# Sparse attention and two MLPs on one core: k and q split once per pair of heads and placed by DMA, x scaled by turned row sums, an order made with slack

## The chip, the cores and the metric

The kernel runs on one core of one Trainium2 chip. The core has TensorE (PE, with its weight loads PEld), VectorE (DVE), ScalarE (ACT), GpSimd (POOL) and SyncE (SP), which issues every DMA here. The metric is the device time of one execution in microseconds; lower is better. Before the change it is 1143.46 us, the median of three runs (1141.05 to 1149.29).

## The reference, cut to what matters

All is in float32, for 4 batches of 8 heads, 576 tokens and head width 64. The result of the attention, 2304 tokens by 512, goes through two MLPs of inner width 2048.

```python
scores = (1.0 / np.sqrt(64)) * np.matmul(q, k.transpose(0, 1, 3, 2))
thresh = np.max(scores, axis=-1, keepdims=True) - tau
scores = np.where(scores >= thresh, scores, -1000000000.0)
attn = np.exp(scores - np.max(scores, axis=-1, keepdims=True))
attn = attn / (np.sum(attn, axis=-1, keepdims=True) + 1e-09)
x = np.matmul(attn, v)                     # then heads side by side: 2304 x 512
h = x @ moe_w_in                           # 512 -> 2048
x = np.where(h > 0.0, h, np.exp(np.minimum(h, 0.0)) - 1.0) @ moe_w_out
h = x @ moe2_w_in
out = np.maximum(0.01 * h, h) @ moe2_w_out
```

## The kernel before, in words

**Exact products from two halves.** TensorE multiplies float32 slowly (two records for each matmul in the trace) and fp32r, a shortened float32, fast. So most operands are split into a high half, which is the value as fp32r, and a low half, the value less its high half. A weight, an activation or an attention weight is then multiplied in two or three fast matmuls. The first heads are not split: up to head `P32` = 9 (not included) the product with v, and up to head `Q32` = 8 the product of q and k, are done in plain float32 (`pv32`, `qk32`).

**Units.** The 32 heads go in 16 pairs. A pair has 9 units of 128 rows of queries: A0 to A3 of its first head, M with the last 64 rows of both heads, and B2, B3, B0, B1 of its second. A unit makes its scores in PSUM tile `s` (in the first 41 units, every other one in `y`), in two halves of 288 keys (L462 in float32, L469 split). VectorE scales them, copies them to `ss` and finds the row's extreme (L477), `thr` is made by VectorE (L482) or POOL (L480), ScalarE masks (L486) and takes the exponential with its row sum `su` (L489, then a read of the sum), VectorE takes the reciprocal (L491), and ScalarE (L306) or POOL (L304) multiplies the whole 128x576 tile `e` by it. TensorE turns `e` in four pieces (L501) and a rest of 64 keys, shared by two units (L516). The turned weights are copied (L568, L569) or split (L546, L549, L553, L556) into `wh`, `wl` and `lt`. When a window of 256 or 320 queries of a head is complete, `pv32` (L587) or `pv` (L606) multiplies with v: nine matmuls for a window, since v's halves lie side by side and give two results in the two halves of PSUM tile `v`.

**After pv.** One half of `v` is copied to `tm`, the other to `x`, each by ScalarE or VectorE, and POOL adds `tm` to `x` (L614, shown under its helper's line L300).

**The halves of k and q.** From head 8 on, `head` loads k and q twice, into both halves of the 128 partitions (L408). POOL makes the high half of k (`k1`, L304) and the low half (`k2`, L300), the high half of q and, in partitions 64 to 127, the low half (L304, L300), for each head anew.

**The first MLP beside the attention.** Six blocks of 256 tokens go through half of the first MLP (8 of 16 slices of the inner width) while the attention of later batches runs (`block` with `reg=True`: L647 makes h, L657 to L674 the activation and its split, L688 y). A block needs x of all heads of its batches (`xready`). The sixteen weight tiles for it are split into halves by POOL, ScalarE and VectorE in the same stretch (L257 to L286). After about 476 us only the MLPs are left, mostly with 512 tokens in a matmul.

**What sets the order.** `Order` is a list scheduler in the program: each operation has a due time (`vt`, in units of `TU`, with offsets in `ST0` and `ST1`), one or more engines that may do it with a cost for each, and the operations and buffers that it waits for. It plays these out once, and what comes out is the fixed order of each engine's queue. On the chip each queue runs in that order: an instruction that waits holds up all that stand behind it on its engine, and SP's queue of DMAs likewise.

## Time and profile before

| | |
|---|---|
| median of three runs | 1143.46 us |
| the profiled execution: its time, its span | 1140.95 us, 1139.2 us |
| PE, PEld busy | 1112.0 us, 940.5 us |
| DVE, ACT, POOL busy | 721.1 us, 665.1 us, 375.9 us |
| granted TensorE clock, mean over the span | 0.993 |
| chain that ended last, shares of the span | PE 76%, ACT 11%, DVE 9%, issue 2%, POOL 1% |
| DMA | 71.52 MB, mean 63 GB/s |

How to read it: busy is the time in which an engine has at least one record open. TensorE's records overlap, since the next matmul starts long before the last record ends, so PE shows 98% although it does not start a matmul as often as it could. What TensorE really loses is seen from the starts of the matmuls: the time from one start to the next, against the shortest time that the same matmul needs when nothing holds it up. The other engines' records do not overlap. The span falls into three stretches: float32 attention alone (to about 124 us), attention with the first MLP beside it (to about 476 us), and the MLPs alone.

### The profile page before, as it was taken

What the parts mean: (1) busy time and instruction counts of PE and PEld (TensorE: products, weight loads), DVE (VectorE), ACT (ScalarE), POOL (GpSimd) and SP (SyncE); (2) the same over time, 40 slices, a digit from 0 to 9 for tenths busy, and PEclk for the clock granted to TensorE, in tenths of its full rate; (3) what the DMA queues carried; (4) which work ended last, traced back from release to release, by engine and by line L of the source; (5) the groups of instructions that cost most, each with busy time, mean ns of one, the idle gap of its engine ahead of it and who ended that gap; (6) DMA issues with size and microseconds to landing.
All of it is one profiled execution on the core that took longest, in us unless ns stands there. A gap on an engine that the chain in (4) does not pass through costs nothing.

```text
span 1139.2 us, 17486 instructions
## 1 busy us (share of the span) xinstructions
PE 1112.0 (98%) x6312; PEld 940.5 (83%) x6312; DVE 721.1 (63%) x1633; ACT 665.1 (58%) x1391; POOL 375.9 (33%) x485
## 2 busy tenths in 40 slices
PE   8999999999999999999999999999999999999998
PEld 4555588999989998889888888988888888888898
DVE  5878788888888887678888643886332322322332
ACT  5888899999999999556545332554322222322222
POOL 3546788889779877101001010010000000000000
PEclk8999999999999999999999999999999999999999
DMA  6333122212122211234434200331010010010010
GB/s 166 108 108 107 37 62 62 84 48 80 52 63 69 81 50 29 75 127 135 161 116 125 93 10 28 93 112 56 1 38 1 1 37 1 1 37 1 1 38 20
DMA packets 37366, 71.52 MB, mean 63 GB/s; under 512 B 9760, under 2 KB 17312, under 8 KB 37280
## 3 DMA queue, kind: packets, MB, share of 16 engines
q1 hardware_dynamic: 37280, 70.40, 20.3%
q8 instruction: 50, 0.82, 0.3%
q14 instruction: 36, 0.29, 0.1%
HBM read 60.95 MB, written 9.44 MB: 62 GB/s over the span
## 4 chain that ended last, share of the span: by engine, by line
PE 76%; ACT 11%; DVE 9%; issue 2%; POOL 1%; POOLq 0%; DVEq 0%; ACTq 0%
PE y L688 31%; PE h L647 16%; PE hb L647 14%; PE v L587 4%; ACT e L489 3%; PE t L501 3%; ACT ss L486 3%; DVE ss L477 2%; PE s L469 2%; ACT wh L546 2%; PE v L606 2%; PE s L462 1%; PE y L462 1%; DVE wl L549 1%; DVE g L659 1%
## 5 line engine op out<-in xcount | busy, mean ns | idle before, releaser
L688 PE MATMUL y<-gh,woh 128*128 128x512 f32 (+1 forms) x736 | 256.8, 349 | 1.6 <-ACT ys L568 1.6
L688 PE MATMUL y<-gl,woh 128*128 128x512 f32 (+1 forms) x736 | 252.3, 343 | 0.0
L688 PE MATMUL y<-gh,wol 128*128 128x512 f32 (+1 forms) x736 | 252.1, 343 | 0.0
L647 PE MATMUL h<-xh,wih 128*128 128x256 f32 (+1 forms) x464 | 157.1, 338 | 3.9 <-DVE g L665 3.6
L688 PEld LDWEIGHTS y<-gh,woh 128*128 128x128 f32 x736 | 139.4, 189 | 18.6 <-ACT ys L568 2.2
L647 PE MATMUL h<-xl,wih 128*128 128x256 f32 (+1 forms) x464 | 153.2, 330 | 0.0
L647 PE MATMUL h<-xh,wil 128*128 128x256 f32 (+1 forms) x464 | 153.1, 330 | 0.0
L688 PEld LDWEIGHTS y<-gl,woh 128*128 128x128 f32 x736 | 139.3, 189 | 16.2
L688 PEld LDWEIGHTS y<-gh,wol 128*128 128x128 f32 x736 | 139.0, 189 | 16.2
L672 ACT CAST gh<-g 128x512 fp32r<-128x512 f32 (+1 forms) x184 | 97.1, 528 | 86.2 <-DVE g L670 46.9
L300 POOL TENSOR_TENSOR xl<-x,xh 128x256 fp32r<-128x256 f32 (+1 forms) x30 | 24.2, 820 | 342.4 <-ACT xh L625 342.4
L299 DVE TENSOR_TENSOR gl<-g,gh 128x512 fp32r<-128x512 f32 (+1 forms) x132 | 85.3, 647 | 54.8 <-ACT gh L672 53.5
L486 ACT ACTIVATE ss<-ss,thr 128x576 f32<-128x576 f32 x144 | 111.5, 775 | 5.8 <-DVE thr L482 3.7
L489 ACT ACTIVATE e<-ss,taun 128x577 f32<-128x577 f32 x144 | 112.0, 778 | 1.5
L477 DVE TENSOR_SCALAR_CACHE_REDUCE ss<-s,scl 128x576 f32<-128x576 f32 x124 | 100.8, 813 | 9.8 <-PE s L462 5.2
L647 PEld LDWEIGHTS h<-xh,wih 128*128 128x128 f32 x464 | 88.1, 190 | 14.4 <-DVE g L665 3.7
L647 PE MATMUL hb<-xl,wih 128*128 128x512 f32 (+1 forms) x272 | 99.1, 364 | 0.0
L647 PE MATMUL hb<-xh,wih 128*128 128x512 f32 (+1 forms) x272 | 99.0, 364 | 0.0
L647 PE MATMUL hb<-xh,wil 128*128 128x512 f32 (+1 forms) x272 | 99.0, 364 | 0.0
L469 PE MATMUL s<-k,qt 128*128 128x288 f32 x472 | 86.6, 306 | 8.4 <-DVE ss L477 8.1
L647 PEld LDWEIGHTS h<-xh,wil 128*128 128x128 f32 x464 | 87.8, 189 | 8.2
L647 PEld LDWEIGHTS h<-xl,wih 128*128 128x128 f32 x464 | 87.7, 189 | 8.1
(538 smaller groups left out, 2124.8 us busy)
## 6 DMA issues: line engine op xcount, KB each, us to landing
wraw<-in_w1i_dram SPq DMA_DIRECT2D x16, 512.0 KB, 4.2
wraw<-in_w1o_dram SPq DMA_DIRECT2D x16, 512.0 KB, 3.5
wraw<-in_w2i_dram SPq DMA_DIRECT2D x16, 512.0 KB, 3.5
wraw<-in_w2o_dram SPq DMA_DIRECT2D x16, 512.0 KB, 3.5
kraw<-in_kT_dram SPq DMA_DIRECT2D x48, 160.0 KB, 2.9
qraw<-in_qT_dram SPq DMA_DIRECT2D x48, 144.0 KB, 2.8
ys<-yp_dram SPq DMA_DIRECT2D x4, 1024.0 KB, 5.5
out_dram<-x SPq DMA_DIRECT2D x16, 256.0 KB, 2.1
```

What stands on the lines that cost most here:

```text
L299: return pick(who, D=(dve(n), lambda: nc.vector.tensor_tensor(**args()), PORT), P=(pool_tt(n), lambda: nc.gpsimd.tensor_tensor(**args())))
L300: P=(pool_tt(n), lambda: nc.gpsimd.tensor_tensor(**args())))
L462: nc.tensor.matmul(s()[n * w:n * w + w, j, 0:HALF], q()[0:64, c:c + w], k()[0:64, k0 + j * HALF:k0 + (j + 1) * HALF], start=True, stop=True)
L469: nc.tensor.matmul(s()[:, j, 0:HALF], q()[:, c:c + 128], kk()[:, k0 + j * HALF:k0 + (j + 1) * HALF], start=(n == 0 and m == 0), stop=(n == ...
L477: o = op((DVE, dve(S) + 60, lambda: nc.vector.tensor_scalar(out=ssr().rearrange("p (j c) -> p j c", j=2), in0=s()[:, :, 0:HALF], scalar1=s ...
L486: o = op((ACT, act(S) + 95, lambda: nc.scalar.activation(out=ssr(), in_=ssr(), func=AF.Prelu, bias=thr(), scale=-1.0, alpha=STEEP)), [ot], ...
L489: o = op((ACT, act(S) + 190, lambda: nc.scalar.activation(out=er(S + 1), in_=ssr(S + 1), func=AF.Exp, bias=taun, accum_out=su())), [o], [s ...
L501: nc.tensor.transpose(t4()[:, c, :], er()[:, c1 + c * 128:c1 + (c + 1) * 128], ident)
L587: nc.tensor.matmul(ps()[0:64, 0:nw], lhs, rhs, start=(c == 0), stop=(c == 4))
L647: nc.tensor.matmul(hp(), w_()[:, cs], x_()[:, 0:tb], start=(k == 0 and z == 0), stop=(k == KC - 1 and z == 2))
L672: o1 = op((ACT, act(tb), lambda: nc.scalar.copy(out=gh()[:, cs], in_=g()[:, cs])), [o], [g, gh], vt)
L688: nc.tensor.matmul(ysl(yg, m), w_()[:, cs], g_()[:, 0:tb], start=(first and z == 0 and share == 0), stop=(last and z == 2 and end))
```

## The change

- `Q32` goes from 8 to 4: heads 4 to 7 also get split k and q.
- k and q of a pair of heads are loaded together into 128 partitions (`kq_pair`), split once by POOL, the low half in place, and twelve DMAs from SBUF to SBUF place the halves where the matmuls want them.
- `e` is no longer multiplied by the reciprocal of its row sum. The sums of a pair's nine units are collected in one tile `su`; TensorE turns it to 9x128, VectorE takes the reciprocal, one DMA stores it in DRAM, three DMAs read it back spread over 64 partitions each, and one 128x576 multiplication by VectorE or POOL scales the pair's part of `x`.
- After `pv`, one half of PSUM tile `v` is copied to `x`, and VectorE adds the other half from PSUM. `tm` is gone.
- In the scheduler an operation of TensorE counts as ready 49.7 ns later, those of the other three engines cost 30 ns more, and latencies count 1.31 times. All due times have other values.

```diff
-P32, Q32 = 9, 8
+P32, Q32 = 9, 4
...
-KN = dict(warm=3, TU=2691.9, hlead=0.875114, hleadb=3.14713, wv0=3.2304, wv1=2.45697, yoff=28639.7, coff=-5493.3,
+KN = dict(margin=49.6784, pad=30.0, late=1.30757, plead=2.02161, warm=3, TU=2594.9, hlead=-1.09928,
+          hleadb=1.51858, wv0=3.7208, wv1=4.27865, yoff=32778.1, coff=-7939.5, NS=41, vlate=-5075.7,
...
-                t = max((d.done + hop(d.eng, e) for d in o.deps), default=0.0)
+                t = max((d.done + hop(d.eng, e) for d in o.deps), default=0.0) + (KN["margin"] if e == PE else 0.0)
...
+            if e in (ACT, DVE, POOL):
+                cost += KN["pad"]
...
+    def kq_pair(p, vt):
+        kr, qr, kh, qh = kraw_r.new(), qraw_r.new(), kh_r.new(), qh_r.new()
+        vt -= KN["plead"] * TU
+        parts = []
+        for r, h, src, n in ((kr, kh, kT, SL), (qr, qh, qT, S)):
+            ld = op((SP, 600, lambda r=r, src=src: nc.sync.dma_start(
+                out=r(), in_=src[2 * p:2 * p + 2].rearrange("g d s -> (g d) s"))), [], [r], vt - 3000, lat=3500)
+            oh = op(hi_of("P", n, h, r), [ld], [r, h], vt)
+            ol = op(tt("P", n, lambda r=r, h=h: dict(
+                out=r().bitcast(F32R), in0=r(), in1=h().bitcast(F32), op=ALU.subtract)), [oh], [r, h], vt)
+            parts.append((oh, ol))
+        (okh, okl), (oqh, oql) = parts
+        for j in range(2):
+            k1, k2, q = k1_r.new(), k2_r.new(), qt_r[j].new()
...
+            for dst, at, cs, src, raw, o in (
+                    (k1, 0, slice(0, SL), kh, 0, okh), (k1, 64, slice(0, SL), kh, 0, okh),
+                    (k2, 0, slice(0, SL), kr, 1, okl), (k2, 64, slice(0, SL), kr, 1, okl),
+                    (q, 0, qs, qh, 0, oqh), (q, 64, qs, qr, 1, oql)):
+                deps.append(op((SP, 600, lambda dst=dst, at=at, cs=cs, src=src, raw=raw, mine=mine: nc.sync.dma_start(
+                    out=dst()[at:at + 64, cs].bitcast(F32), in_=src()[mine] if raw else src()[mine].bitcast(F32))),
+                    [o], [src, dst], vt + 1500 + 5 * TU * j, lat=3000))
...
-        o = op((DVE, 75, lambda: nc.vector.reciprocal(out=rs(), in_=su())), [o], [su, rs], vt + so["rec"])
-        o = op(hi_of("PA", S, er, er, rs), [o], [e, rs], vt + so["norm"])
...
+    def row_sums(p, vt):
+        (su, done), rb, rt, ps = sums.pop(p), rb_r.new(), rt_r.new(), v_ps.new()
+        o = op((PE, 107, lambda: nc.tensor.transpose(ps()[0:NU, 0:128], su(), ident)), done, [su, ps], vt)
+        o = op((DVE, dve(128), lambda: nc.vector.reciprocal(out=rt(), in_=ps()[0:NU, 0:128])), [o], [ps, rt], vt)
+        o = op((SP, 600, lambda: nc.sync.dma_start(out=rsd[p].rearrange("(c p) -> c p", p=128), in_=rt())),
+               [o], [rt], vt, lat=2500)
+        got = []
+        for a, c, r, n in ((0, 0, 0, S), (64, 0, S + 64, 512), (64, 512, S, 64)):
+            got.append(op((SP, 600, lambda a=a, c=c, r=r, n=n: nc.sync.dma_start(
+                out=rb()[a:a + 64, c:c + n], in_=rsd[p, r:r + n].partition_broadcast(64))), [o], [rb], vt, lat=3000))
...
+        xready[bt, hp] = [op(tt("DP", S, lambda: dict(out=xs, in0=xs, in1=rb(), op=ALU.mult)),
+                             [*got, *waits.pop((bt, hp))], [rb], vt + 9000)]
...
-        half = [op(copy_of("AD", nw, lambda: tm()[a:a + 64, 0:nw], lambda: ps()[z:z + 64, 0:nw]), [o], [ps, tm], vt),
-                op(copy_of("AD", nw, lambda: x[a:a + 64, hp, cols], lambda: ps()[a:a + 64, 0:nw]), [o], [ps], vt)]
-        o = op(tt("P", nw, lambda: dict(out=x[a:a + 64, hp, cols], in0=x[a:a + 64, hp, cols],
-                                        in1=tm()[a:a + 64, 0:nw], op=ALU.add)), half, [tm], vt)
+        o1 = op(copy_of("AD", nw, lambda: x[a:a + 64, hp, cols], lambda: ps()[z:z + 64, 0:nw]), [o], [ps], vt)
+        o = op((DVE, dve(nw), lambda: nc.vector.tensor_tensor(
+            out=x[a:a + 64, hp, cols], in0=ps()[a:a + 64, 0:nw], in1=x[a:a + 64, hp, cols], op=ALU.add)),
```

**What moves on TensorE.** The first two lists stand in the middle of the attention: s, t and v are the attention's (scores, turned weights, product with v), h and y the MLP's. Before:

```order
1564 L647 MATMUL h<-xh_4348,wih_1084 128x256
1565 L647 MATMUL h<-xl_4366,wih_1084 128x256
1566 L647 MATMUL h<-xh_4348,wil_1100 128x256
1567 L647 MATMUL h<-xh_4373,wih_1084 128x256
1568 L647 MATMUL h<-xl_4385,wih_1084 128x256
1569 L647 MATMUL h<-xh_4373,wil_1100 128x256
1570 L469 MATMUL s<-k_4821,qt_90 128x288
1571 L469 MATMUL s<-k_4873,qt_90 128x288
1572 L469 MATMUL s<-k_4821,qt_90 128x288
1573 L469 MATMUL s<-k_4873,qt_90 128x288
1574 L501 MATMUL t<-ident,e_92 128x128 x4
1575 L516 MATMUL t<-ident,e_92 128x128
```

And now, at a like place (L696 is h, L495 the scores, L655 the product with v):

```order
1578 L655 MATMUL v<-wh,v 128x320
1579 L495 MATMUL s<-k_4305,qt_89 128x288
1580 L495 MATMUL s<-k_4340,qt_89 128x288
1581 L655 MATMUL v<-wl,v 128x320
1582 L655 MATMUL v<-wh,v 128x320
1583 L655 MATMUL v<-wl,v 128x320
1584 L495 MATMUL s<-k_4305,qt_89 128x288
1585 L495 MATMUL s<-k_4340,qt_89 128x288
1586 L655 MATMUL v<-wh,v 128x320
1587 L655 MATMUL v<-wl,v 128x320
1588 L655 MATMUL v<-lt,v 128x320
1589 L696 MATMUL h<-xh_4105,wih_1013 128x256
```

The kinds of work now alternate in shorter pieces: up to the first matmul of 512 tokens TensorE's queue changes from one line of the program to another 602 times before and 971 times now.

**What moves on SP.** The queue of DMAs in the middle of the attention, before (k and q of one head in two DMAs each, v in one):

```order
79 L408 DMA kraw<-in_kT_dram 64x640 x2
80 L408 DMA qraw<-in_qT_dram 64x576 x2
81 L408 DMA kraw<-in_kT_dram 64x640 x2
82 L389 DMA vraw<-in_vm_dram 128x320
83 L408 DMA qraw<-in_qT_dram 64x576 x2
```

And now, for one pair of heads: two loads, the row sums of an earlier pair out and back (rsd, rb), and the first head's six placements with the beginning of the second's:

```order
114 L423 DMA kraw<-in_kT_dram 128x640
115 L423 DMA qraw<-in_qT_dram 128x576
116 L540 DMA rsd_dram<-rt 9x128
117 L544 DMA rb<-rsd_dram 64x576
118 L544 DMA rb<-rsd_dram 64x512
119 L544 DMA rb<-rsd_dram 64x64
120 L438 DMA k_2142<-kh 64x640 x2
121 L438 DMA k_2166<-kraw 64x640 x2
122 L438 DMA qt_89<-qh 64x576
123 L438 DMA qt_89<-qraw 64x576
124 L397 DMA vraw<-in_vm_dram 128x320
125 L438 DMA k_2333<-kh 64x640 x2
```

The placements stand behind the row sums' way through DRAM in the same queue; in some pairs they stand ahead of it. SP's queue has 178 rows before and 335 now.

**What moves on POOL.** Before, in the middle of the attention:

```order
226 L300 TENSOR_TENSOR x<-x,tm 64x320
227 L304 TENSOR_SCALAR e_92<-e_92,rs 128x576
228 L304 TENSOR_SCALAR v<-vraw 128x5x64
229 L304 TENSOR_SCALAR k_3457<-kraw 128x640
230 L300 TENSOR_TENSOR v<-vraw,v 128x5x64
231 L300 TENSOR_TENSOR k_3481<-kraw,k_3457 128x640
232 L300 TENSOR_TENSOR gl<-g,gh 128x256
233 L661 TENSOR_SCALAR g<-g 128x256
234 L304 TENSOR_SCALAR qt_90<-qraw 128x576
235 L304 TENSOR_SCALAR e_91<-e_91,rs 128x576
```

And now:

```order
170 L506 TENSOR_SCALAR thr<-nm,taup 128x1
171 L308 TENSOR_SCALAR v<-vraw 128x5x64
172 L304 TENSOR_TENSOR v<-vraw,v 128x5x64
173 L506 TENSOR_SCALAR thr<-nm,taup 128x1
174 L304 TENSOR_TENSOR gl<-g,gh 128x256
175 L506 TENSOR_SCALAR thr<-nm,taup 128x1
176 L304 TENSOR_TENSOR x<-x,rb 128x576
177 L710 TENSOR_SCALAR g<-g 128x256
```

The multiplications of e and the additions of tm are gone from POOL's queue. Over the whole attention POOL makes 78 of the thresholds (35 before) and 14 of the 16 multiplications of x, and it splits k and q 14 times in place of 24.

## Rows read from the trace of the kernel before

**Rows 1.** Windows by stretch: start:end, length, then busy us of each engine
```profile
core 0: us, PE busy (x) PEld busy (x) DVE busy (x) ACT busy (x) POOL busy (x), PEclk, DMA share, GB/s
160.00:476.00 316.00, 302.81 (x2341) 289.01 (x2340) 260.97 (x708) 289.56 (x691) 253.63 (x336) 1.00 0.21 62
476.00:1139.20 663.20, 658.46 (x3276) 560.99 (x3274) 339.95 (x595) 244.66 (x438) 30.43 (x32) 1.00 0.17 54
```
**Rows 2.** Groups by line, PE, 160 to 476 us: count | busy, mean | idle before, releaser
```profile
L469 PE MATMUL s<-k,qt 128*128 128x288 f32 x410 | 75.1, 305 | 6.4 <-DVE ss L477 6.1
L647 PE MATMUL h<-xh,wih 128*128 128x256 f32 (+1 forms) x188 | 57.1, 304 | 3.9 <-DVE g L665 3.6
L501 PE MATMUL t<-ident,e 128*128 128x128 f32 x384 | 56.4, 273 | 1.2 <-DVE wl L549 1.1
L688 PE MATMUL y<-gh,woh 128*128 128x256 f32 x180 | 55.0, 306 | 0.9 <-ACT ys L568 0.9
...
L606 PE MATMUL v<-wh,v 128*128 128x320 f32 (+1 forms) x172 | 48.7, 305 | 0.0
...
L516 PE MATMUL t<-ident,e 128*128 128x128 f32 (+1 forms) x54 | 15.4, 286 | 0.7 <-DVE wl L549 0.5
```
**Rows 3.** Timeline of PE, single places: start us, length of the merged records, what
```profile
9.59 1.24 PE L462 MATMUL s<-k,k 64*128 64x288 f32 x4
10.66 1.14 PE L462 MATMUL y<-k,k 64*128 64x288 f32 x4
...
443.61 0.69 PE L469 MATMUL s<-k,qt 128*128 128x288 f32 x4
444.14 0.60 PE L501 MATMUL t<-ident,e 128*128 128x128 f32 x4
444.57 0.27 PE L516 MATMUL t<-ident,e 128*128 128x128 f32 x1
...
461.07 0.28 PE L606 MATMUL v<-wh,v 128*128 128x256 f32 x1
462.15 0.28 PE L688 MATMUL y<-gh,woh 128*128 128x256 f32 x1
```
**Rows 4.** Windows, the second, third and fourth pair of heads, columns as in the first group
```profile
37.90:72.70 34.80, 33.81 (x140) 18.07 (x138) 26.41 (x71) 26.54 (x53) 16.98 (x21) 0.90 0.34 103
72.70:99.50 26.80, 26.71 (x122) 14.91 (x121) 20.97 (x58) 24.29 (x50) 13.97 (x18) 1.00 0.40 115
99.50:124.40 24.90, 24.20 (x116) 13.59 (x114) 20.18 (x53) 21.77 (x44) 16.85 (x21) 1.00 0.29 83
```
**Rows 5.** Windows of PE alone: length, busy (x), granted clock, DMA share, GB/s
```profile
55.00:60.00 5.00, 5.00 (x14) 0.50 0.00 0
```
**Rows 6.** Timeline of PE just before: start, length, what, idle before it
```profile
54.09 1.38 PE L462 MATMUL s<-k,k 64*128 64x288 f32 x4 [0.99 <-DVE ss L477]
```
**Rows 7.** Groups by line, whole span: count | busy us, mean ns | idle before
```profile
L304 POOL TENSOR_SCALAR e<-e,rs 128x576 f32<-128x576 f32 x88 | 68.0, 773 | 25.0 <-DVE rs L491 21.8 <-PE s L469 1.3
...
L306 ACT ACTIVATE e<-e,rs 128x576 f32<-128x576 f32 x56 | 43.0, 772 | 4.0 <-DVE rs L491 3.8
...
L300 POOL TENSOR_TENSOR k<-kraw,k 128x640 fp32r<-128x640 f32 x24 | 37.9, 1579 | 0.3
...
L300 POOL TENSOR_TENSOR x<-x,tm 64x320 f32<-64x320 f32 (+1 forms) x46 | 36.8, 801 | 17.3 <-ACT x L568 8.2 <-DVE x L569 6.6 <-DVE rs L491 1.1
```
**Rows 8.** Groups by line and form, DVE, 0 to 460 us, then 480 to 1139 us
```profile
L659 DVE TENSOR_SCALAR g<-g 128x256 f32<-128x256 f32 x24 | 19.8, 825 | 4.2 <-ACT g L657 4.0
...
L659 DVE TENSOR_SCALAR g<-g 128x256 f32<-128x256 f32 x16 | 4.6, 289 | 3.6 <-ACT g L657 3.6
```
**Rows 9.** DMA issues of the page: queue, count, KB each, median us to landing
```profile
kraw<-in_kT_dram SPq DMA_DIRECT2D x48, 160.0 KB, 2.9
...
vraw<-in_vm_dram SPq DMA_DIRECT2D x23, 160.0 KB, 2.2
```
**Rows 10.** Timeline of SP's queue: start us, us for the issues, what
```profile
206.10 1.11 SPq L408 DMA_DIRECT2D kraw<-in_kT_dram  x2
```

More of the change, by code (lines that the diff above doesn't have):

```diff
@@ L171, in run @@
                 port = start + cost
-            o.eng, o.done = e, start + cost + o.lat
+            o.eng, o.done = e, start + cost + o.lat * KN["late"]
             free[e] = start + cost
@@ L213, in attn_moe_kernel @@
 @with_exitstack
-def attn_moe_kernel(ctx, tc, qT, kT, vm, tau, w1i, w1o, w2i, w2o, yp, out):
+def attn_moe_kernel(ctx, tc, qT, kT, vm, tau, w1i, w1o, w2i, w2o, yp, rsd, out):
     nc = tc.nc
@@ L328, in attn_moe_kernel @@
     lt_r = ring(ap_, 2, [128, WIN[1]], F32R, "lt")
-    tm_r = ring(ap_, 1, [128, WIN[1]], F32, "tm")
-    sm_r = {t: ring(ap_, 4, [128, 1], F32, t) for t in ("nm", "thr", "su", "rs")}
+    sm_r = {t: ring(ap_, 4, [128, 1], F32, t) for t in ("nm", "thr")}
+    su_r = ring(ap_, 3, [128, NU], F32, "su")
+    rt_r = ring(ap_, 1, [NU, 128], F32, "rt")
+    rb_r = ring(ap_, 1, [128, S], F32, "rb")
     s_r = ring(psa, 1, [128, 2, 512], F32, "s")
@@ L401, in head @@
             return
-        kr, qr = kraw_r.new(), qraw_r.new()
-        k1, k2, q = k1_r.new(), k2_r.new(), qt_r[par].new()
-        qs = slice(64 * par, 64 * par + S)
-        def load2(dst, src):
-            for j in range(2):
-                nc.sync.dma_start(out=dst()[64 * j:64 * j + 64, 0:src.shape[2]], in_=src[g])
-        lk = op((SP, 1200, lambda: load2(kr, kT)), [], [kr], vt - 3000, lat=3000)
-        lq = op((SP, 1200, lambda: load2(qr, qT)), [], [qr], vt - 3000, lat=3000)
-        o1 = op(hi_of("P", SL, k1, kr), [lk], [kr, k1], vt)
@@ L413, in head @@
-        o2 = op(tt("P", SL, lambda: dict(out=k2(), in0=kr(), in1=k1().bitcast(F32), op=ALU.subtract)),
-                [o1], [kr, k1, k2], vt)
-        o3 = op(hi_of("P", S, lambda: q()[:, qs], lambda: qr()[:, 0:S]), [lq], [qr, q], vt)
-        o4 = op(tt("P", S, lambda: dict(
-            out=q()[64:128, qs], in0=qr()[64:128, 0:S], in1=q()[64:128, qs].bitcast(F32), op=ALU.subtract)),
-            [o3], [qr, q], vt)
-        heads[g] = (k1, k2, q, v, (o2, o4), ov)
+        if not par:
+            kq_pair(g // 2, vt)
@@ new lines, in head @@
+        k1, k2, q, deps = kqs.pop(g)
+        heads[g] = (k1, k2, q, v, deps, ov)
+    kqs = {}
+    def kq_pair(p, vt):
[12 more added lines that the diff above has]
+            k1, k2, q = k1_r.new(), k2_r.new(), qt_r[j].new()
+            mine, qs = slice(64 * j, 64 * j + 64), slice(64 * j, 64 * j + S)
+            deps = []
+            for dst, at, cs, src, raw, o in (
[5 more added lines that the diff above has]
+                    [o], [src, dst], vt + 1500 + 5 * TU * j, lat=3000))
+            kqs[2 * p + j] = (k1, k2, q, deps)
@@ L421, in attn_moe_kernel @@
     pair, turned = [None], []
-    wins, left = {}, {}
+    wins, left, sums, rbs, waits = {}, {}, {}, {}, {}
     xready = {}
@@ L453, in ssr @@
             return ss()[:, 1:S + 1] if n == S else ss()[:, side:side + S + 1]
-        nm, thr, su, rs = (sm_r[t].new() for t in ("nm", "thr", "su", "rs"))
+        nm, thr = (sm_r[t].new() for t in ("nm", "thr"))
+        n9 = u % NU
+        if n9 == 0:
+            sums[p] = (su_r.new(), [])
+        su, col = sums[p][0], COLS.index(name)
         hd = [heads[pc[0]] for pc in pieces]
@@ L489, in unit @@
         o = op((ACT, act(S) + 190, lambda: nc.scalar.activation(
-            out=er(S + 1), in_=ssr(S + 1), func=AF.Exp, bias=taun, accum_out=su())), [o], [ss, e, su], vt + so["exp"])
-        o = op((DVE, 75, lambda: nc.vector.reciprocal(out=rs(), in_=su())), [o], [su, rs], vt + so["rec"])
-        o = op(hi_of("PA", S, er, er, rs), [o], [e, rs], vt + so["norm"])
+            out=er(S + 1), in_=ssr(S + 1), func=AF.Exp, bias=taun, accum_out=su()[:, col:col + 1])), [o], [ss, e, su], vt + so["exp"])
+        sums[p][1].append(o)
+        if n9 == NU - 1:
+            row_sums(p, vt + so["rec"])
         t, c1 = t_r.new(), 64 if side else 0
@@ L592, in pv32 @@
         o = op(copy_of("AD", nw, lambda: x[a:a + 64, hp, cols], lambda: ps()[0:64, 0:nw]), [o], [ps], vt)
-        xready.setdefault((bt, hp), []).append(o)
+        waits.setdefault((bt, hp), []).append(o)
     def pv(g, w, vt):
@@ L599, in pv @@
         v, ov = heads[g][3], heads[g][5]
-        ps, tm = v_ps.new(), tm_r.new()
+        ps = v_ps.new()
         ops = [(v, c, y, c) for c in range(4) for y in (wh, wl)] + [(v, 4, lt, None)]
```

27 lines of the change are left out of this document (20 added, 7 removed).

## The prediction, made before the changed kernel was run

> **What bounds the kernel now.** I read the windows by stretch first. In the last stretch, 476 us to the end, TensorE is busy 658.5 of 663.2 us at full clock [rows 1]; the change leaves the MLPs' work there as it is, so its gain or loss lies in the first 476 us. There I ask how much of the time TensorE starts matmuls as fast as it can. The timeline gives the shortest times: four split score matmuls go from 443.61 to 444.14, 0.53 us; four turns from 444.14 to 444.57, 0.43; nine matmuls of a 256 window from 461.07 to 462.15, 1.08, so 0.12 for one of 256 columns [rows 3]. A 320 window I estimate by its columns at 1.35. The groups by line give the counts from 160 to 476 us [rows 2]: 410 score matmuls (54 us), 384 and 54 turns (47), 172 products with wh, thus 43 windows (52), and three times 188 and three times 180 MLP matmuls (132). That is 286 us of work in a stretch of 316: **some 30 us are lost**, of which the page shows 13.2 as idle [rows 1], because TensorE's records are longer than its steps. The idle that shows stands mostly before the scores, for VectorE's pass over s (6.1 us), and before h, for VectorE's activation (3.6) [rows 2]. ACT is busy for 290 of these 316 us, DVE for 261, POOL for 254 [rows 1]: no engine has much room, and a late step on one is soon felt on TensorE.
>
> In the float32 part the windows by pair of heads show 34.8, 26.8 and 24.9 us for the second, third and fourth pair, which do the same work [rows 4]. The second was granted a clock of 0.90. Between 55 and 60 us the clock is 0.50, the lower of its two levels, after a wait of 0.99 us for VectorE [rows 5, 6].
>
> **The change, part by part.** The sum is made against the profiled execution, 1140.95 us; the median of the runs stands 2.5 us above it, and I add that at the end.
>
> *Scores of heads 4 to 7 in split form.* A float32 unit takes 1.07 us from its first half to the next unit (9.59 to 10.66), a split one 0.53 [rows 3]. With eight whole units in a pair and two pairs, 16 x 0.54 = 8.6 us of TensorE time; for the M units, with two short pieces in float32, I count nothing. It stands in a part where no MLP work can yet fill in, so it is a gain only if nothing else bounds the pair. The fourth pair's 24.9 us would become 20.6. ACT has 21.8 us there [rows 4], less the normalization: 56 of 144 are on ACT at 0.772 us [rows 7], 3.5 a pair, 2.7 us, which leaves 19.1. That is close below 20.6, so I take 7.5 us, with 4 and 8.6 as ends.
>
> *The normalization of e goes.* ACT loses 43.0 us, POOL 68.0 [rows 7], and the chain of a unit from exponential to turn loses a reciprocal and a pass of 0.77 us. None of it is a gain by itself; it makes room.
>
> *k and q once per pair.* POOL splits 14 times in place of 24; the low half of k alone takes 1.579 us [rows 7], so ten times 1.6 us, 16 us, and as much again and more for the other three pieces, which are of like size: 40 us as an estimate. In exchange SP issues twelve placements a pair. Two issues take 1.11 us [rows 10], so these take 6.7 us of a queue that had four long double issues a pair.
>
> *The sum of the halves.* POOL loses 36.8 us of additions [rows 7], VectorE gets 46 additions for 32 copies that it made to tm: about even. The copy and the addition now follow each other, and PSUM tile v is held longer by one step, about half of the 0.8 us that POOL's addition took; windows come 43 in 316 us [rows 1, 2], one in 7 us, which covers it.
>
> *Row sums.* 16 turns on TensorE at 0.107 [rows 3]: +1.7 us. The way through DRAM is a store and a load. Loads of 160 KB land in 2.2 to 2.9 us [rows 9], so with four issues about 8 us; x needs it only when a block starts. At the end of the attention the same number of TensorE rows (79 each) stands between the last product with v and the first 512-wide matmul as before; that covers it, and were it uncovered it would cost up to these 8 us once. The Trainium skill, "DMA: Bandwidth & Descriptors", section "Bandwidth", says that transfers under 64 KB are dominated by a fixed cost (about 2 us), and to batch to 1 MiB, which speaks against 4 KB stores and 160 KB placements. No row here is of so small a store; by that page the way would be about 4 us, an estimate, and the sum would not change.
>
> *What the room is worth.* With e, the halves and the additions gone POOL has some 130 us less (new: 43 more thresholds and 14 products with x). VectorE gains without losing work: the same 128x256 step of the activation takes 825 ns while POOL is busy and 289 ns later [rows 8], 24 x 0.54 = 13 us, and it is in the chain that h waits for. The order now puts MLP and v matmuls in between the attention's steps in pieces of three, and counts 30 to 50 ns of slack for each operation. How much of the 30 us this takes back no row shows. The ends are 0 (the waits go elsewhere) and 22, where 8 us remain, since some waits are of the kind that the order did not foresee. I take 11, about a third, near the 9.7 that the two largest waits for VectorE sum to [rows 2].
>
> *Pairs one and two.* The second pair takes 9.9 us more than the fourth [rows 4]. Weights are now due every 4.28 units in place of 2.46, and the chain is shorter. I take 3 us; the ends are 10 gained and 4 lost.
>
> Sum: 7.5 + 11 + 3 - 1.7 = 19.8 us; 1140.95 - 19.8 = 1121.2, and with the 2.5 us of the median **1124 us**.
>
> **The rivals.**
>
> *The waits stay (B).* Only TensorE's work falls, 7.5 - 1.7, and the time is about 1138. For it: VectorE, which most waits name, loses only small steps and gets the addition. Against it: the 13 us of rows 8.
>
> *The waits nearly vanish (C).* 7.5 + 22 + 6 - 1.7 = 34 us, about 1110. For it: ACT and POOL both get over a tenth of their time free. Against it: in the stretch before 124 us nothing fills TensorE's gaps.
>
> *The placements come late (D), and it is slower.* A head's k and q can be placed only when the last scores of the head two before are made, four units before it starts: 4/9 of 24.9 us [rows 4], 11.1 us. Six issues at 0.55 and a landing of 2.9 [rows 9, 10] make 6.2 us. If SP stands behind the row sums' store, waits for its landing and issues three loads first, it is 0.55 + 2.9 + 1.7 = 5.2 us more, 11.4: just past the limit, so it decides where both meet and landings are slower than these. If it does in each of 14 pairs, and TensorE stands for one unit, 2.8 us, the cost is 39 us: 1124 + 39 = 1163. Against it: in many pairs the loads of the row sums stand behind the first head's placements or well ahead of them.
>
> *The clock falls in pairs three and four (E).* There TensorE gets less work and more gaps. Five us at the lower level cost 2.5 [rows 5]; four such falls cost 10: 1134. The Trainium skill, "TensorE: Matmul & The Clock Gate", Part 1, has it that the clock is throttled by default and released by activity. The trace agrees where the clock falls after a wait [rows 6]; it stays at 1.00 from 160 to 476 us [rows 1], with matmuls of the fast kind throughout.
>
> **How the numbers follow.** The forecast gets 0.57 and C 0.13; both are faster. B gets 0.14 and E 0.05, both within 1%. D, with whatever else makes the new order wait, gets 0.11. A measurement of this kernel tells about 1%, 11.4 us, from no change. So 0.70 faster, 0.19 the same, 0.11 slower. All the better ends together give 8.6 + 22 + 10 - 1.7 = 39 us, 1104; all the worse 4 + 0 - 4 - 1.7, 1145. The range leaves out D and the last of C: **1108 to 1143**.
>
> **What would show it.** In the changed profile the scores of pairs three and four should stand under the split line, these pairs take about 21 us, ACT and POOL be busy some 45 and 130 us less, the stretch of MLPs alone begin near 456 us instead of 476, and the last stretch be as long as before. The 128x256 step should fall well below 825 ns. If TensorE waits for DMA at the first scores of a pair, D holds; if its idle time in the mixed stretch stays near 13 us, B. I am wrong if ACT or VectorE paces pairs three and four, or if the finer order only changes which engine TensorE waits for.

## The result, and the profile after

The changed kernel takes **1124.28 us**, the median of four runs (1122.48 to 1132.26); the kernel before, run beside it, 1142.45 us. The ratio is 0.9845, with a 95% interval of 0.9813 to 0.9877. The forecast was 1124 us, in a range of 1108 to 1143. The execution at 1132.26 us was granted a mean clock of 0.99, the other three 1.00. The profiled execution took 1122.48 us, 18.5 less than the one before.

The page of the changed kernel, first its busy times, then the shares of the chain that ended last:

```profile
PE 1103.0 (98%) x6328; PEld 932.4 (83%) x6328; DVE 712.3 (64%) x1467; ACT 622.3 (56%) x1315; POOL 285.0 (25%) x385
...
PE 91%; DVE 5%; ACT 3%; issue 1%; DVEq 0%; ACTq 0%
```

ACT lost 43 us of work and POOL 91; TensorE now carries 91% of the chain in place of 76%. The windows of the changed kernel, with the columns of [rows 1]: the second, third and fourth pair; the mixed and the last stretch.

```profile
32.90:62.30 29.40, 29.40 (x125) 13.78 (x124) 19.93 (x47) 21.52 (x46) 10.96 (x15) 1.00 0.51 134
62.30:89.00 26.70, 26.63 (x127) 14.62 (x126) 17.84 (x41) 19.63 (x42) 14.21 (x19) 1.00 0.64 164
89.00:113.10 24.10, 23.83 (x119) 13.66 (x118) 18.68 (x42) 19.38 (x42) 12.81 (x15) 1.00 0.58 145
...
160.00:456.00 296.00, 288.12 (x2305) 281.63 (x2304) 251.50 (x603) 257.61 (x622) 156.76 (x236) 1.00 0.45 117
456.00:1120.70 664.70, 661.14 (x3281) 562.18 (x3279) 344.78 (x591) 245.80 (x440) 49.27 (x45) 1.00 0.17 54
```

Against [rows 4], the second pair is 5.4 us shorter, at a full clock, but the third and fourth together only 0.9: 50.8 us where the forecast had some 42 to 44. TensorE is busy in nearly all of their time, ACT in 19.4 of the fourth's 24.1. So neither ACT nor a wait bounds them, and yet all of their scores got cheaper. The last stretch is as before.

Groups of TensorE's instructions in the mixed stretch, 160 to 456 us (count | busy us, mean ns | idle before, releaser):

```profile
L495 PE MATMUL s<-k,qt 128*128 128x288 f32 x404 | 74.8, 297 | 0.2
...
L696 PE MATMUL h<-xh,wih 128*128 128x256 f32 x180 | 56.0, 311 | 0.6 <-DVE g L714 0.6
L737 PE MATMUL y<-gh,woh 128*128 128x256 f32 x178 | 54.7, 307 | 1.2 <-DVE ys L618 0.9 <-ACT ys L617 0.2
L655 PE MATMUL v<-wh,v 128*128 128x320 f32 (+1 forms) x172 | 51.4, 306 | 5.2 <-DVE rt L539 3.5 <-DVE g L708 0.8 <-ACT wh L595 0.5
```

TensorE's idle time before the scores fell from 6.4 to 0.2 us and that before h from 3.9 to 0.6 [rows 2]; most of it had been waits for VectorE. A new wait stands before the product with v (L655): the row sums are turned in the product's PSUM tile, and it is free only after VectorE's reciprocal of them (L539).

**Where TensorE's time went.** For each two matmuls that follow each other I take the time from start to start, less the shortest time of the first one's kind (score 0.133 us split and 0.243 float32, turn 0.107, product with v 0.120 or 0.147 split and 0.216 or 0.270 float32, h and y of 256 tokens 0.120). The short float32 scores of the M units start in twos, and two of them count 0.245. The sum is lost time. The three places begin at the first exponential of the first, third and fifth pair; the last ends at the first matmul of 512 tokens. Length / lost, in us of the profiled executions:

| kernel | median us | pairs 1, 2 | pairs 3, 4 | pair 5 to the end of the attention |
|---|---|---|---|---|
| before | 1142.3 | 62.1 / 18.0 | 51.7 / 8.5 | 348.5 / 35.3 |
| changed | 1124.3 | 52.3 / 13.3 | 50.8 / 12.1 | 342.4 / 24.4 |
| changed, no slack | 1123.6 | 51.1 / 10.6 | 43.9 / 4.6 | 346.5 / 31.8 |
| float32 product whole | 1114.0 | 49.0 / 8.9 | 47.5 / 7.5 | 338.2 / 22.6 |
| whole, heads 4–7 float32 | 1121.3 | 49.0 / 9.6 | 53.9 / 7.9 | 341.3 / 23.5 |
| float32 product on 128 columns | 1108.0 | 47.6 / 8.4 | 43.4 / 4.5 | 339.0 / 21.4 |
| e normalized again | 1136.8 | 60.8 / 22.3 | 50.5 / 11.1 | 345.0 / 28.3 |
| k, q per head | 1128.6 | 52.6 / 12.7 | 51.3 / 12.4 | 348.6 / 31.1 |
| and halves added by POOL | 1138.2 | 52.7 / 12.7 | 51.3 / 12.4 | 356.5 / 38.9 |

Three things are to be seen in the first two rows. The mixed stretch lost 10.9 us less, where the forecast had taken 11. In pairs three and four the matmuls' shortest times fell by 4.6 us (from 43.3 to 38.7) while lost time rose by 3.6. And pairs one and two are 9.8 us shorter, but lost time is only 4.6 of that: they hold 5.1 us less work, most of it float32 products with v and scores of the third pair that now stand later, and the mixed part holds 4.8 us more. So a place's length alone does not say what a part of the change was worth.

### The profile page after: what moved, and what is told of

Same layout as the page of the kernel before. It is cut to its first block, busy times and chain, and to the rows that moved or that the text cites. A ratio compares the mean times of both kernels' runs of the same rounds, so it can differ in the third digit from the quotient of the medians.

```text
span 1120.7 us, 17435 instructions
## 1 busy us (share of the span) xinstructions
PE 1103.0 (98%) x6328; PEld 932.4 (83%) x6328; DVE 712.3 (64%) x1467; ACT 622.3 (56%) x1315; POOL 285.0 (25%) x385
## 4 chain that ended last, share of the span: by engine, by line
PE 91%; DVE 5%; ACT 3%; issue 1%; DVEq 0%; ACTq 0%
PE y L737 34%; PE h L696 19%; PE hb L696 15%; PE v L636 5%; PE s L495 5%; PE v L655 5%; PE t L528 5%; DVE ss L503 1%; ACT e L515 1%; PE s L488 1%; DVE rt L539 1%; PE y L495 1%; PE y L488 1%; DVE wl L598 1%; ACT ss L512 1%
## 5 line engine op out<-in xcount | busy, mean ns | idle before, releaser
L696 PE MATMUL h<-xh,wih 128*128 128x256 f32 (+1 forms) x464 | 158.8, 342 | 1.0 <-DVE g L714 1.0
L696 PE MATMUL h<-xh,wil 128*128 128x256 f32 (+1 forms) x464 | 153.2, 330 | 0.0
L696 PE MATMUL h<-xl,wih 128*128 128x256 f32 (+1 forms) x464 | 153.1, 330 | 0.0
L737 PEld LDWEIGHTS y<-gh,wol 128*128 128x128 f32 x736 | 139.0, 189 | 16.3
L303 DVE TENSOR_TENSOR gl<-g,gh 128x512 fp32r<-128x512 f32 (+1 forms) x129 | 84.2, 652 | 52.8 <-ACT gh L721 51.7
L304 POOL TENSOR_TENSOR xl<-x,xh 128x256 fp32r<-128x256 f32 (+1 forms) x32 | 27.9, 884 | 290.3 <-ACT xh L674 290.3
L696 PE MATMUL hb<-xh,wih 128*128 128x512 f32 (+1 forms) x272 | 99.1, 364 | 0.0
L495 PE MATMUL s<-k,qt 128*128 128x288 f32 x512 | 97.8, 302 | 1.3 <-DVE ss L503 1.1
L696 PE MATMUL hb<-xl,wih 128*128 128x512 f32 (+1 forms) x272 | 99.1, 364 | 0.0
L696 PE MATMUL hb<-xh,wil 128*128 128x512 f32 (+1 forms) x272 | 99.0, 364 | 0.0
L696 PEld LDWEIGHTS h<-xh,wih 128*128 128x128 f32 x464 | 87.5, 189 | 10.2 <-ACT lt L602 0.8
L696 PEld LDWEIGHTS h<-xl,wih 128*128 128x128 f32 x464 | 87.7, 189 | 8.5 <-POOL xl L304 0.2
L696 PEld LDWEIGHTS h<-xh,wil 128*128 128x128 f32 x464 | 87.5, 189 | 8.1
```

Of the source, the lines that this page charges most:

```text
L303: return pick(who, D=(dve(n), lambda: nc.vector.tensor_tensor(**args()), PORT), P=(pool_tt(n), lambda: nc.gpsimd.tensor_tensor(**args())))
L304: P=(pool_tt(n), lambda: nc.gpsimd.tensor_tensor(**args())))
L495: nc.tensor.matmul(s()[:, j, 0:HALF], q()[:, c:c + 128], kk()[:, k0 + j * HALF:k0 + (j + 1) * HALF], start=(n == 0 and m == 0), stop=(n == ...
L696: nc.tensor.matmul(hp(), w_()[:, cs], x_()[:, 0:tb], start=(k == 0 and z == 0), stop=(k == KC - 1 and z == 2))
L737: nc.tensor.matmul(ysl(yg, m), w_()[:, cs], g_()[:, 0:tb], start=(first and z == 0 and share == 0), stop=(last and z == 2 and end))
```

## The experiments

The kernel before, run beside each of them, took 1142.18 to 1142.63 us. Ratios are to it.

### Is it the room or the slack? Two orders

The changed kernel without slack:

```diff
-KN = dict(margin=49.6784, pad=30.0, late=1.30757, ...
+KN = dict(margin=0.0, pad=0.0, late=1.0, ...
```

> The changed kernel with the three numbers of slack taken out of the order's costs (margin 0, pad 0, latencies times 1.0); every operation of the change stays. Theory 'room' (less work on ACT, POOL and VectorE is what takes TensorE's waits away from 160 to 455 us): the lost time there stays near the 14 us of the changed kernel and the run is at 1122 to 1129 us. Theory 'slack' (the order with slack does it): the lost time goes back towards 29 us and the run to 1133 to 1140 us.

Measured: 1123.64 us, ratio 0.9832 (0.9808 to 0.9855), the same time as with slack: the time is where 'room' had it, the lost time of the mixed stretch where 'slack' had it. By the table slack takes 7.4 us of lost time out of the mixed stretch and puts 7.5 into pairs three and four and 2.7 into one and two. Without slack these two later pairs take 43.9 us, what the forecast had for them, and the attention ends 3.7 us earlier. The stretch of the MLPs alone then takes that back: without slack it has a wait and a clock fall near its start, which the changed kernel does not have there. A row of PE's timeline, and a window of PE (length, busy, granted clock, DMA share, GB/s):

```profile
479.54 0.50 PE L737 MATMUL y<-gl,woh 128*128 128x512 f32 x1 [2.21 <-DVE gl L303]
480.00:485.00 5.00, 5.00 (x17) 0.66 0.52 151
```

The same slack in the kernel before:

```diff
-KN = dict(warm=3, TU=2691.9, ...
+KN = dict(margin=49.6784, pad=30.0, late=1.30757, warm=3, TU=2691.9, ...
...
-                t = max((d.done + hop(d.eng, e) for d in o.deps), default=0.0)
+                t = max((d.done + hop(d.eng, e) for d in o.deps), default=0.0) + (KN["margin"] if e == PE else 0.0)
...
```

> The kernel before with the same slack in its order's costs (margin 49.7 ns, pad 30 ns, latencies times 1.31), and nothing else of the change. Theory 'slack': 1127 to 1134 us, lost time in the mixed stretch about 15 us instead of 29. Theory 'room': ACT and POOL are as full as before, and it stays within 1138 to 1148 us.

Measured: 1151.96 us, ratio 1.0073 (1.0049 to 1.0098). By the same reckoning its mixed part loses 30.0 us (35.3 without slack), its first four pairs 43.1 (26.4). Part of that is a long clock fall; windows of PE in this kernel (length, busy, granted clock, DMA share, GB/s):

```profile
15.00:20.00 5.00, 5.00 (x13) 0.50 0.61 190
...
30.00:35.00 5.00, 3.44 (x10) 0.50 0.26 82
...
45.00:50.00 5.00, 5.00 (x23) 1.00 0.14 33
```

So slack is no gain in itself. In both kernels it takes lost time out of the mixed part (5.3 us here, 7.4 in the changed kernel) and puts more into the first four pairs (16.7 and 10.2).

A third kernel was meant to have another order, with a unit of due time 0.1% longer:

```diff
-          ... plead=2.02161, warm=3, TU=2594.9, ...
+          ... plead=2.02161, warm=3, TU=2597.5, ...
```

> The changed kernel with all due times stretched by 0.1% (TU 2597.5 instead of 2594.9): the same operations in another order that the scheduler finds as good. It tells how much the accident of one order is worth. If it is small: 1122 to 1128 us; if much of the gain lies in this one order: 1130 us and more.

Measured: 1124.8 us, 0.9837 (0.9811 to 0.9863). But all due times grew alike and the queues came out row by row the same, so it tells nothing of other orders; it is a second measurement of the changed kernel, 0.5 us from the first.

### What the finer order costs in float32

With slack the scheduler puts other work between the five matmuls of the float32 product with v (`pv32`). First, the five as one operation:

```diff
-        o = None
-        for c in range(5):
-            o = op((PE, mm32(nw), lambda c=c: mms(c)), [o, ov, *ready], [ps, v, wh, lt], vt)
+        o = op((PE, 5 * mm32(nw), lambda: [mms(c) for c in range(5)]), [ov, *ready], [ps, v, wh, lt], vt)
```

> The changed kernel with the float32 product with v of a window (five matmuls) as one piece of the order, so that nothing can stand between its matmuls. Theory 'switches' (in the first 113 us each change of TensorE between float32 and the fast kinds costs 0.13 to 0.2 us, and the finer order of the change made 95 of them where pairs three and four had 58): those two pairs get 4 to 6 us shorter and the run is at 1115 to 1120 us. Rival (the pieces in between only fill time in which TensorE would wait anyway): the pairs keep their 51 us, 1123 to 1128 us.

Measured: **1114.01 us**, 0.9746 (0.9723 to 0.9769): 10.3 us faster than the changed kernel and 1 us below the theory's range, though pairs three and four got only 3.3 us shorter where it had 4 to 6; the other places gained as well. The changes of kind are what cost, then; but is it float32 that is dear to enter and leave? Two kernels put the scores of heads 4 to 7 back in float32, one with the product in pieces as in the change, one with it whole:

```diff
-P32, Q32 = 9, 4
+P32, Q32 = 9, 8
```

> The changed kernel with the scores of heads 4 to 7 back in float32, in one piece with nothing else changed. Theory 'switches': the split scores save 8.6 us of TensorE's shortest times in pairs three and four, but the finer order makes TensorE change between float32 products with v and split scores dozens of times, 0.13 us each; with the scores in float32 too, those changes go. So the two cancel and the time is 1124 to 1128 us, with pairs three and four together at 50 to 54 us (50.8 in the changed kernel). Rival 'the scores are worth their sum': the 7.5 us of the forecast come back, 1130 to 1133 us.

> The changed kernel with the float32 product with v in one piece and the scores of heads 4 to 7 back in float32. Beside the kernel with the product in one piece alone (1114.0 us) it shows what split scores are worth where TensorE changes kind seldom. Theory 'switches': their shortest times now count nearly in full, 6 to 9 us, so 1120 to 1123 us, and pairs three and four take some 4 us each more than there. Rival 'ACT or VectorE paces these pairs': the scores are hidden beside other work and the time stays at 1114 to 1117 us.

Measured: 1134.92 us in pieces (0.9925, 0.9898 to 0.9952) and 1121.33 whole (0.9804, 0.9764 to 0.9844). The first falls outside my theory and just past its rival: although scores and product are now both float32, each change between them still costs. Its profiled execution, 1143.85 us, has a clock of 0.50 from 15 to 30 us, so I read only the later places; rows of PE's timeline in the third pair:

```profile
87.64 0.75 PE L488 MATMUL s<-k,k 64*128 64x288 f32 x2
88.32 0.65 PE L636 MATMUL v<-wh,v 128*64 128x256 f32 x2
88.90 0.75 PE L488 MATMUL s<-k,k 64*128 64x288 f32 x2
```

Two records of the scores need 0.49 us and take 0.68 here, two of the product need 0.43 and take 0.58. By the starts of the single records a change costs 0.14 us into the product and 0.20 out of it. The other kernel, with the product whole, shows the scores' worth where changes are few: 7.3 us, against 7.5 forecast; pairs three and four take 6.4 us more than with split scores. Float32 against fp32r was thus the wrong line. What else differs is the tile form, the first numbers in these groups of the changed kernel (the product, the split scores, the float32 scores; min/median/max ns, first and last start, forms):

```profile
L636 PE MATMUL v<-wh,v x144: 379/432/484, 14.0 to 135.8; 128*64 128x256 f32 x72, 128*64 128x320 f32 x72
...
L495 PE MATMUL s<-k,qt x512: 288/295/406, 56.7 to 431.0; 128*128 128x288 f32 x171
...
L488 PE MATMUL s<-k,k x40: 402/403/507, 6.4 to 52.5; 64*128 64x288 f32 x32, 64*64 64x288 f32 x8
```

The product uses 64 of 128 columns, the float32 scores 64 of 128 rows, the split matmuls both in full. So the product was given 128 columns, v being loaded into both halves of its tile (the upper half of the result is not read):

```diff
-            ov = op((SP, 600, lambda: nc.sync.dma_start(out=v()[:, :, 0:D], in_=vm[g])), [], [v], vt + KN["vlate"],
+            def load2():
+                for z in (0, D):
+                    nc.sync.dma_start(out=v()[:, :, z:z + D], in_=vm[g])
+
+            ov = op((SP, 600, load2), [], [v], vt + KN["vlate"], lat=3000)
...
-            lhs, rhs = ((v()[:, c, 0:D], wh()[:, c, 0:nw]) if c < 4 else
+            lhs, rhs = ((v()[:, c], wh()[:, c, 0:nw]) if c < 4 else
...
-            nc.tensor.matmul(ps()[0:64, 0:nw], lhs, rhs, start=(c == 0), stop=(c == 4))
+            nc.tensor.matmul(ps()[:, 0:nw], lhs, rhs, start=(c == 0), stop=(c == 4))
```

> The changed kernel, with the float32 product with v made over all 128 columns of TensorE (v is loaded into both halves of its tile; the upper half of the result is not used). The order stays as it is. In the changed kernel each change from or to this product costs TensorE 0.13 to 0.2 us. Theory 'the tile form': the loss comes where a 128x64 tile follows a tile of 128 rows by 128 columns, so most of the changes with the split scores and the turns become free and the time falls to 1114 to 1119 us. Rival 'float32': the loss comes where float32 work meets anything else or a short piece of itself, whatever its width, and the time stays at 1122 to 1127 us.

Measured: **1108.00 us** (1107.74 to 1108.18), 0.9698 (0.9683 to 0.9712), the fastest of all, 16.3 us below the changed kernel, and beyond what its theory expected. The same matmuls stand in the same order in both; the timeline of PE in the changed kernel, third pair (start us, length of the merged records, what):

```profile
62.38 0.53 PE L495 MATMUL s<-k,qt 128*128 128x288 f32 x2
62.84 0.75 PE L636 MATMUL v<-wh,v 128*64 128x320 f32 x2
63.52 0.66 PE L528 MATMUL t<-ident,e 128*128 128x128 f32 x4
64.11 0.75 PE L636 MATMUL v<-wh,v 128*64 128x320 f32 x2
64.80 0.33 PE L565 MATMUL h<-ident,e 128*128 128x128 f32 x1
65.05 0.75 PE L636 MATMUL v<-wh,v 128*64 128x320 f32 x2
65.73 0.53 PE L495 MATMUL y<-k,qt 128*128 128x288 f32 x2
66.19 0.75 PE L636 MATMUL v<-lt,v 64*64 64x320 f32 x2
66.87 0.54 PE L495 MATMUL y<-k,qt 128*128 128x288 f32 x2
```

and with the product on 128 columns:

```profile
58.32 0.67 PE L498 MATMUL s<-k,qt 128*128 128x288 f32 x2
58.82 0.70 PE L639 MATMUL v<-wh,v 128*128 128x320 f32 x2
59.36 0.60 PE L531 MATMUL t<-ident,e 128*128 128x128 f32 x4
59.80 0.70 PE L639 MATMUL v<-wh,v 128*128 128x320 f32 x2
60.34 0.27 PE L568 MATMUL h<-ident,e 128*128 128x128 f32 x1
60.45 0.70 PE L639 MATMUL v<-wh,v 128*128 128x320 f32 x2
60.74 0.66 PE L498 MATMUL y<-k,qt 128*128 128x288 f32 x2
61.34 0.80 PE L639 MATMUL v<-lt,v 64*128 64x320 f32 x2
62.07 0.53 PE L498 MATMUL y<-k,qt 128*128 128x288 f32 x2
```

Neither shows a wait, and PE is busy throughout. Two products and the change to the turns take 0.68 us (62.84 to 63.52) and then 0.54 (58.82 to 59.36), which is twice the 0.27 of one. From the first row to the last it is 4.49 us and then 3.75. Over pairs three and four both have 95 changes from one line to another; the pairs lose 12.1 us in the one and 4.5 in the other. Of these 4.5 some 2.8 stand at the 16 changes to and from the product's rest of 64 keys, which still uses 64 of 128 rows (61.34 in the list). So in one kernel the same float32 product is free to enter on 128x128 and costs on 64x128: the tile form decides, not float32. The Trainium skill, "TensorEngine Tiling (Array Packing)", section "Tiling Modes", says that a change of the tiling mode drains TensorE. These rows agree: by the starts, 0.14 to 0.20 us for each change in the changed kernel. I had not weighed that rule in the prediction.

### Each part undone

The normalization in each unit again, without row sums and scaling of x:

```diff
+        o = op((DVE, 75, lambda: nc.vector.reciprocal(out=rs(), in_=su())), [o], [su, rs], vt + so["exp"])
+        o = op(hi_of("PA", S, er, er, rs), [o], [e, rs], vt + so["exp"])
...
-        if u % NU == NU - 1:
-            scaled(*divmod(u // NU, H // 2))
```

> The changed kernel with the exponentials normalized in each unit again (a reciprocal by VectorE and a 128x576 multiplication by ScalarE or POOL, 144 of them, about 111 us of these engines), without the turned row sums, their way through DRAM and the scaling of x. Theory 'room and a short chain': ACT is full again beside the MLP, waits return in the stretch from 160 to 456 us and TensorE's clock falls again in the first two pairs; 8 to 16 us are lost and 2 to 5 won by the row sums' 16 turns and the wait for their PSUM tile, so 1130 to 1138 us. Rival 'slack hides it': TensorE's queue has slack for the longer chain and the row sums cost what they save, 1121 to 1127 us.

Measured: 1136.81 us, 0.9940 (0.9914 to 0.9967), as the theory had it. Of the 11 us in its profiled execution 8.5 lie in pairs one and two. Windows of PE there, this kernel and then the changed one:

```profile
10.00:15.00 5.00, 2.58 (x10) 0.89 1.02 201
15.00:20.00 5.00, 5.00 (x16) 0.50 0.38 100
20.00:25.00 5.00, 5.00 (x13) 0.50 0.63 202
25.00:30.00 5.00, 5.00 (x13) 0.50 0.00 0
```

```profile
10.00:15.00 5.00, 3.89 (x23) 1.00 1.00 245
15.00:20.00 5.00, 5.00 (x22) 1.00 0.68 191
20.00:25.00 5.00, 5.00 (x26) 1.00 0.49 146
```

The waits that precede the fall, from the timeline of PE of the kernel with the normalization back (idle before it, releaser):

```profile
12.80 0.70 PE L481 MATMUL s<-k,k 64*64 64x288 f32 x2 [1.09 <-DVE ss L496]
14.83 1.19 PE L481 MATMUL s<-k,k 64*64 64x288 f32 x2 [1.33 <-DMA k<-in_qT_dram]
```

Between 10 and 15 us TensorE is idle for 2.42 us here and 1.11 in the changed kernel; then the clock falls to the lower of its two levels, or does not. One of these waits is for a DMA, so this is not the chain of the unit alone. Nor is the normalization needed for such a fall: `e4_q32_8`, above, has one in the same place without it. The times show that the kernel with the normalization back is slower; that the longer chain is what lowers its clock is argued.

Then k and q loaded and split per head by POOL, in place of `kq_pair`:

```diff
-        if not par:
-            kq_pair(g // 2, vt)
-        k1, k2, q, deps = kqs.pop(g)
...
+        o1 = op(hi_of("P", SL, k1, kr), [lk], [kr, k1], vt)
+        o2 = op(tt("P", SL, lambda: dict(out=k2(), in0=kr(), in1=k1().bitcast(F32), op=ALU.subtract)),
+                [o1], [kr, k1, k2], vt)
...
```

> The changed kernel with k and q loaded twice and split for each head by POOL, as before, and no placements by DMA (POOL gets some 75 us more work over heads 4 to 31, SP's queue 168 placements less). Theory 'POOL is off the path': POOL is busy for little over half of the stretch from 160 to 456 us, so this costs only through the SBUF side that POOL shares with VectorE: 1124 to 1128 us. Rival 'POOL and VectorE hold each other up': VectorE's 128x256 step of the activation rises towards the 825 ns of before, waits for g and ss return, 1130 to 1136 us. Rival 'placements are late': without them the time falls below 1121 us.

Measured: 1128.61 us, 0.9865 (0.9819 to 0.9910). That interval overlaps the changed kernel's, so the 4.3 us are likely but not shown by the times; the table puts 6.7 us more lost time in the mixed part. POOL is busy 193 us from 160 to 456, in place of 157, and yet VectorE's 128x256 step takes 556 ns up to 445 us, against 529 in the changed kernel. So the time ends just above what the first theory gave, the second's mechanism does not show, and placements that come late are excluded.

On top of that, the halves added by POOL from a copy in `tm`:

```diff
-        o1 = op(copy_of("AD", nw, lambda: x[a:a + 64, hp, cols], lambda: ps()[z:z + 64, 0:nw]), [o], [ps], vt)
...
+        half = [op(copy_of("AD", nw, lambda: tm()[a:a + 64, 0:nw], lambda: ps()[z:z + 64, 0:nw]), [o], [ps, tm], vt),
+                op(copy_of("AD", nw, lambda: x[a:a + 64, hp, cols], lambda: ps()[a:a + 64, 0:nw]), [o], [ps], vt)]
...
```

> The kernel with k and q split per head by POOL (1128.6 us), with the halves of the product with v added by POOL from a copy in SBUF again, as before (POOL gets 46 additions of 0.8 us, 37 us; VectorE loses as many additions and gets back some of the copies). Theory 'POOL holds up VectorE through their shared side, and the product's tile comes free later or sooner by half a microsecond': 1127 to 1131 us, no more than 0.3% either way. Rival 'the addition by VectorE was part of the gain': 1132 to 1138 us, since POOL then stands before x and holds up VectorE longer.

Measured: 1138.16 us, 0.9965 (0.9952 to 0.9979): 9.6 us slower than without it, at the upper end of the rival. The traces point to another mechanism than I wrote there. The scheduler gives the copies to ScalarE; ACT's copies out of v, 160 to 456 us, in this kernel:

```profile
L603 ACT COPY x<-v 64x256 f32<-64x256 f32 (+1 forms) x25 | 9.7, 390 | 7.1 <-DVE tm L604 6.7
...
L603 ACT COPY tm<-v 64x256 f32<-64x256 f32 (+1 forms) x17 | 6.7, 393 | 2.2 <-PE v L641 0.9 <-POOL gl L304 0.8
```

and with the addition by VectorE:

```profile
L602 ACT COPY x<-v 64x256 f32<-64x256 f32 (+1 forms) x11 | 4.3, 392 | 1.9 <-PE v L640 1.6
```

ScalarE makes 42 copies in place of 11, and VectorE's split of the turned weights, which needs ScalarE's half first, waits 12.3 us for it in place of 5.8. TensorE in its turn waits 3.0 us for that split (1.0 without) and 4.3 for VectorE's pass over the scores (1.7). No run isolates this, so it is argued:

```profile
L584 DVE TENSOR_TENSOR wl<-t,wh 128x512 fp32r<-128x512 f32 (+1 forms) x102 | 63.5, 632 | 13.1 <-ACT wh L581 12.3
```

### Two that moved nothing

Both start from the kernel with the float32 product whole. Slack only after 120 us of planned time:

```diff
+SLACK = 1.2e5
...
+                t += KN["margin"] if e == PE and t > SLACK else 0.0
...
-            if e in (ACT, DVE, POOL):
+            if e in (ACT, DVE, POOL) and start > SLACK:
...
```

> The kernel with the float32 product with v in one piece (1114.0 us), with the three slacks of the order only after the first 120 us of the planned time. Theory 'slack cuts work into short pieces, which costs in float32 and pays beside the MLP': without it the first pairs lose less and the mixed stretch keeps its 14 us of lost time, so 1108 to 1113 us. Rival 'one piece has already cured it': 1113 to 1116 us. Rival 'slack is also what keeps the clock up early': clock falls in the first pairs and 1116 to 1124 us.

Measured: 1113.78 us, 0.9740 (0.9721 to 0.9760). The row sums in the ring of `t`:

```diff
-        (su, done), rb, rt, ps = sums.pop(p), rb_r.new(), rt_r.new(), v_ps.new()
+        (su, done), rb, rt, ps = sums.pop(p), rb_r.new(), rt_r.new(), t_r.new()
```

> The kernel with the float32 product with v in one piece (1114.0 us), with the turned row sums in the two-buffer PSUM ring of the turned weights instead of the single tile of the product with v. Theory 'the row sums hold the product's tile': the waits of the product with v for the reciprocal (3.5 us in 160 to 456 us of the changed kernel) go and the time falls by 2 to 4 us, to 1110 to 1112 us. Rival 'it only moves': the turns wait for the reciprocal in its place, 1113 to 1116 us.

Measured: 1113.22 us, 0.9743 (0.9729 to 0.9758). In both the rival holds: once the product is whole, leaving out the early slack gains nothing (its profile has a short clock fall, 0.83 from 15 to 25 us, so a gain of 1 or 2 us could be hidden); and the wait for the reciprocal only moves. TensorE's waits from 160 to 447 us in the last kernel (in all us, times, longest); the product with v waited 4.2 us for `rt` without the edit:

```profile
PE s L495 <- DVE ss L503: 1.8, 4, 0.8
PE h L695 <- DVE g L713: 1.7, 5, 0.6
PE t L565 <- DVE rt L539: 1.3, 4, 0.5
```

## Why the prediction was right

The time was right to a third of a microsecond, and that is partly luck. By kind of time the 18.5 us between the profiled executions are: 4.9 less of shortest times (5.8 forecast, the scores less the row sums), 4.6 less lost in pairs one and two (3), 10.9 in the mixed part (11), 1.7 before the first and after the last place (nothing), and against them 3.6 more lost in pairs three and four (nothing). So the sum left out a cost, and gains larger than forecast made up for most of it. The profiled time came out 1.3 us above the 1121.2 of the sum, and the median 1.8 above that, where I had added 2.5.

- **Scores of heads 4 to 7** (7.5 us forecast): the size is right, 7.3 us between the two kernels with the product whole; at the shortest times it is 6.9, since the 1.07 us that I read for a float32 unit are four records of 0.243 and 0.1 of lost time. But pairs three and four gave only 0.9. The step that failed is "so it is a gain only if nothing else bounds the pair": I looked for ACT as that bound, and the bound was TensorE itself, in a cost that I had left out. I quoted the finer alternation of the order (602 changes, then 971) and priced only its gain. With the product on 128 columns these pairs take 43.4 us, what was forecast, and lose 4.5 in place of 12.1.
- **Pairs one and two** (3 us, ends -4 and 10): 9.8 us by length, but 4.6 in lost time; most of the rest is work that moved. The clock falls of before [rows 5] are gone in the profiled execution. I took them to come from the unit's chain; one returns with the normalization, but one comes without it too, so that mechanism is likely and not shown.
- **The room** (11 us of some 30 lost): lost time in the mixed part fell by 10.9 of 35.3 us. But 7.4 of it is there only with the slack, and room alone gives 3.5. The waits for ss and g went as expected, and the 128x256 step of [rows 8] fell to 529 ns (0 to 445 us):

```profile
L708 DVE TENSOR_SCALAR g<-g 128x256 f32<-128x256 f32 x19 | 10.0, 529 | 1.3 <-ACT g L706 0.9
```

- **Row sums** (-1.7): the sixteen turns are there at 0.107 us. The way through DRAM takes 7.8 us in the first pair, from the store's issue at 40.26 to the last landing at 48.09, as the sum had it and twice the other estimate of 4; "that covers it" holds for it. But the turned sums' hold on the product's tile was missed, 3.5 us of idle time; a turn of 0.1 us is followed by a reciprocal of 0.95.
- **The sum of the halves** ("about even"): wrong. It is worth 9.6 us where POOL has the most work, by the traces through ScalarE's copies. **k and q once per pair** cost POOL 37 us less in the mixed stretch (40 estimated) and are worth perhaps 4 us.
- **Rivals.** D did not come: in the trace no first score waits for a DMA, and the placements land in 2.5 and 2.9 us:

```profile
k<-kh SPq DMA_DIRECT2D x56, 160.0 KB, 2.5
k<-kraw SPq DMA_DIRECT2D x56, 160.0 KB, 2.9
```

  E did not come, the clock is 1.00 in pairs three and four. B is out, since the waits fell. C's time is reached with the product on 128 columns, which is not C's mechanism: there too the mixed part still loses 21.4 us.

The parts undone one at a time (10.6, 12.5, 4.3 and 9.6 us) and the finer order's cost (10.3) leave 26.7 us, more than the 18.2 measured, so they overlap; how they share it stays open. Three things were not tried: the float32 scores with full rows, the product's rest of 64 keys with full rows, and 128 columns with the slack taken out.
